# Later attention units: k and q transposed in place, their low parts subtracted by GpSimd

## The chip, the core and the metric

The kernel runs on one core of one Trainium2 chip. The metric is device microseconds of one execution. Three runs of the kernel before took 695.42, 696.80 and 697.27 us: a median of 696.8 us.

## What is computed

Inputs are q, k and v of 4 batches x 8 heads x 768 positions x 64, and two weight matrices, 512 x 2048 and 2048 x 512, stored as 64-bit floats. First comes a linear attention with a decay for each head, then a two-layer network with softplus:

```python
for t in range(S):
    state = gamma[None, :, None, None] * state + np.einsum('bhd,bhe->bhde', k[:, :, t], v[:, :, t])
    y[:, :, t] = scale * np.einsum('bhd,bhde->bhe', q[:, :, t], state)
x = np.ascontiguousarray(y.transpose(0, 2, 1, 3)).reshape(B * S, H * D)
h = x @ w_in
g = np.maximum(h, 0.0) + np.log1p(np.exp(-np.abs(h)))
out = (g @ w_out).astype(np.float32)
```

## The kernel before

**Attention by units.** A unit is 128 positions (a chunk) of four of the eight heads: 4 batches x 6 chunks x 2 halves = 48 units. The recurrence is done chunk by chunk: scores of the chunk (`sc`), masked to the lower triangle (`ah`, `al`), times v, plus q times the state that the chunks before left (`st`); the sum is `yp`, and the state grows by k times v (`stp`). The decays are multiplied into q and v beforehand by GpSimd (L166 or L162, and L167). The first chunk of a batch has no state to read.

**Hi and lo parts.** TensorE multiplies most things as fp32r, a shortened fp32. A value is split into a rounded high part (a cast on ACT) and a low part (value minus high part), and a product is three products: high-high, high-low, low-high. The first 12 units do without this in attention (their k and q are transposed by TensorE, L176). The 36 later units, those that the change touches, load k and q a second time as blocks of 32 x 32 (`kb`, `qb`: 16 DMAs of 16 KB for a unit, L136), so that DVE's 32 x 32 transpose puts each block in its place.

**A later unit, before.** DVE transposes `kb` and `qb` into one PSUM tile `tp` (L184). ACT casts high parts of k and q into `kq` (L187, L188), which has two buffers, `kq0` and `kq1`, for even and odd units; DVE subtracts to get the low parts (L190, L191). `kq` index 0 holds k (high part on a head's own 64 partitions, low part on the other 64), index 1 q's high part on both, index 2 q's low part. TensorE makes the scores in two steps of two heads (L212); ACT and DVE split them (L214 to L216); GpSimd masks `ah`, then `al` (L218); TensorE makes `yp` (L284 to L288); ACT and DVE split it into the ring `xh`, `xl` (L290, L292), from which the first layer reads.

**PSUM.** `tp`, the two `sc` tiles and `yp` of a unit all come from one pool with two buffers of one bank each, taken in turn in the order in which the program asks: `sc`, `sc`, `tp` of the next unit, `yp`.

**The two layers.** Rows are processed in nine blocks (2 x 256, 6 x 384, 256). A step makes 512 columns' worth of the hidden layer: 12 products `hp` for a 384 block (L320 to L322), a softplus chain DVE, ACT, DVE (L327, L328, L332), the split (ACT `gh` L334, GpSimd `gl` L336), and two steps later nine products `acc` of the second layer (L351 to L353). `hp` has two buffers. A block's first two steps can do half of their `hp` products before the last unit of the block has its `yp`, and the other half after.

**The order.** The program emits the parts of a unit at ticks between the steps, and Tile's scheduler, which runs its own timeline, sets the order of each engine's queue. Each engine then works through its queue in that order, and an instruction that waits holds what stands behind it. All the large loads are issued by SP's queue (SyncE), in one order as well. A block tile has two buffers, so the blocks of a unit can be loaded when those of the unit two earlier are free.

Of the kernel before, what the change touches and what calls it, by code (L numbers as in the profile page):

```python
# [10 lines left out]
F32 = mybir.dt.float32  # L11
# [4 lines left out]
ALU = mybir.AluOpType  # L16

P = 128
C = 128
# [14 lines left out]
def decay_attention_then_softplus_ffn(ctx: ExitStack, tc: tile.TileContext, q, k, v, w_in, w_out, qtab, vtab, gtab, out):  # L34
    nc = tc.nc
# [9 lines left out]
    NJ = HH // 2  # L45
# [6 lines left out]
    ps_a = ctx.enter_context(tc.tile_pool(name="ps_a", bufs=2, space=bass.MemoryType.PSUM))  # L52
# [116 lines left out]
    def operands(n):  # L169
        b, c, hf = units[n]  # L170
        kn, *rest, vn = loads.pop(n)
        tp = ps_a.tile([P, 2, NJ, C], F32, name="tp", tag="a")
        if n < WHOLE:
            for t, x in enumerate((kn, *rest)):
                for j in range(NJ):
                    nc.tensor.transpose(tp[:, t, j, :], x[:, 2 * j:2 * j + 2, :], ident)  # L176
            qt = qs[:, n % 2]
            nc.scalar.copy(kz[lo, 0], tp[lo, 0])
            nc.vector.tensor_copy(kz[up, 1], tp[up, 0])
            nc.scalar.copy(qt, tp[:, 1])  # L180
            live[n] = [qt, kn, vn]
            return
        for t, x in enumerate(rest):
            nc.vector.transpose(tp[:, t].rearrange("p j c -> p (j c)"), x.rearrange("p m i d -> p (m i d)"))  # L184
        kq = kqs[n % 2]
        for par, own, oth in sides:
            nc.scalar.copy(kq[own, :2, par], tp[own])  # L187
            nc.scalar.copy(kq[oth, 1, par], tp[own, 1])  # L188
        for par, own, oth in sides:
            nc.vector.tensor_tensor(kq[oth, 0, par], tp[own, 0], kq[own, 0, par].bitcast(F32), op=ALU.subtract)  # L190
            nc.vector.tensor_tensor(kq[own, 2, par], tp[own, 1], kq[own, 1, par].bitcast(F32), op=ALU.subtract)  # L191

        vhl = attn.tile([P, HH, 2, D], F32R, name="vhl", tag="vhl", bufs=2)
        nc.scalar.copy(vhl[:, :, 0, :], vn)
        nc.vector.tensor_tensor(vhl[:, :, 1, :], vn, vhl[:, :, 0, :].bitcast(F32), op=ALU.subtract)
        live[n] = [kq, vhl, kn, vn]
# [100 lines left out]


    PARTS = {-6: load_unit, -2: decay, 0: operands, 2: scores, 3: new_state, 5: stack_and_outputs}
    FIRST_TICK = min(PARTS)  # L300
    PERIOD = 4
# [72 lines left out]
    for i, a, b in turns:  # L374
        m = WIDE // BLOCKS[i]
# [64 lines left out]
    for a, b in zip(starts, starts[1:]):  # L440
        i = steps[b][0]
        if i == 2:
            a = b - SPREAD
        have = ticks_for(i - 1)
        for s in range(a, b):

            t, n = (s - a + 1, b - a) if i == 2 else (min(s - a, b - a - 2), b - a - 2)
# [59 lines left out]
```

## Time and profile before

| | before |
|---|---|
| median of 3 runs | 696.8 us (695.42 to 697.27) |
| profiled execution | 699.58 us, span 697.8 us |
| TensorE busy | 663.9 us, 95% of the span |
| VectorE (DVE) busy | 419.7 us, 60% |
| ScalarE (ACT) busy | 343.4 us, 49% |
| GpSimd (POOL) busy | 283.1 us, 41% |
| DMA | 47.53 MB, mean 68 GB/s |

The profile names engines PE (TensorE products), PEld (its weight loads), DVE, ACT, POOL and SP. A row of a group gives the line of the kernel, the engine and operation, output <- inputs, shapes and count, then busy us and mean ns of one, then how long the engine stood idle just before and what ended that. A row of the timeline gives start, duration, and in brackets the idle time before and its releaser. TensorE's products overlap: the distance between two starts, not the duration, is what one costs in a dense stretch. The first 100 us load and convert the weights; the later units run from about 110 us to 610 us; then only the two layers are left.

### The profile page before, as it was taken

The page shows a single profiled execution, that of the slowest core. Times are in us where ns is not written, and L with a number is a line of the kernel's source. Part 1 is how long each engine was busy: PE and PEld are TensorE (multiplying, and loading weights), DVE is VectorE, ACT ScalarE, POOL GpSimd, SP SyncE. Part 2 cuts the span into 40 slices and gives each one's busy share as a digit, 9 for nine tenths or more (in the row PEclk, how much of TensorE's full clock was granted, in tenths as well). Part 3 has the DMA queues.
Part 4 walks back from the last instruction along what each step waited for, and adds up shares of the span by engine and source line. Part 5 has one row for each costly group of instructions (what it writes and reads, how often), then busy time and mean ns, then how long its engine had stood idle before and what let it go on. Part 6 is the DMA issues. An engine that isn't in the chain of part 4 may idle for free.

```text
span 697.8 us, 12577 instructions
## 1 busy us (share of the span) xinstructions
PE 663.9 (95%) x4136; PEld 602.5 (86%) x4136; DVE 419.7 (60%) x915; ACT 343.4 (49%) x772; POOL 283.1 (41%) x354
## 2 busy tenths in 40 slices
PE   5798899999999999998999979999899998999997
PEld 4787899998999889997999879998799988999996
DVE  5675777567556676666666666664865666543321
ACT  4866766455445455454444455443644536432221
POOL 5766677333333244333333424343243324222221
PEclk9998999999999999999999999999999999999999
DMA  8788750232112331122212232122221231000100
GB/s 245 210 217 230 213 167 23 41 85 64 35 33 40 75 80 36 25 44 72 38 33 43 37 95 56 22 45 40 74 37 33 41 73 41 1 1 1 46 0 31
DMA packets 156993, 47.53 MB, mean 68 GB/s; under 512 B 143616, under 2 KB 151808, under 8 KB 156928
## 3 DMA queue, kind: packets, MB, share of 16 engines
q1 hardware_dynamic: 156480, 46.72, 28.0%
q8 instruction: 33, 0.54, 0.3%
q14 instruction: 32, 0.26, 0.1%
q10 hardware_dynamic: 448, 0.01, 0.0%
HBM read 40.39 MB, written 6.29 MB: 67 GB/s over the span
## 4 chain that ended last, share of the span: by engine, by line
PE 82%; DMA 7%; DVE 3%; ACT 3%; SPq 2%; POOL 1%; issue 1%; DVEq 0%; POOLq 0%; ACTq 0%
PE hp L320 12%; PE hp L322 12%; PE hp L321 12%; PE acc L352 12%; PE acc L351 12%; PE acc L353 11%; PE sc L212 2%; PE stp L235 2%; DMA win<-in_moe_w_in_dram 2%; DMA wout<-in_moe_w_out_dram 2%; PE yp L287 1%; DMA vn<-in_v_dram 1%; SPq L136 1%; PE yp L288 1%; PE yp L286 1%
## 5 line engine op out<-in xcount | busy, mean ns | idle before, releaser
L336 POOL TENSOR_TENSOR gl<-sp,gh 128x384 fp32r<-128x384 f32 (+1 forms) x120 | 128.7, 1074 | 174.4 <-ACT gh L334 157.7
L320 PE MATMUL hp<-xh,winhl 128*128 128x384 f32 (+1 forms) x576 | 187.8, 328 | 2.9 <-DMA out_dram<-o 2.4
L322 PE MATMUL hp<-xh,winhl 128*128 128x384 f32 (+1 forms) x576 | 185.9, 323 | 0.3 <-POOL winhl L99 0.3
L321 PE MATMUL hp<-xl,winhl 128*128 128x384 f32 (+1 forms) x576 | 185.3, 322 | 0.0
L351 PE MATMUL acc<-wouthl,gh 128*128 128x512 f32 x384 | 151.3, 395 | 0.0
L352 PE MATMUL acc<-wouthl,gh 128*128 128x512 f32 x384 | 151.3, 394 | 0.0
L353 PE MATMUL acc<-wouthl,gl 128*128 128x512 f32 x384 | 147.9, 395 | 0.1
L327 DVE TENSOR_SCALAR sp<-hp 128x384 uint32<-128x384 uint32 (+1 forms) x120 | 69.2, 578 | 95.6 <-PE hp L322 90.0
L328 ACT ACTIVATE sp<-sp 128x384 f32<-128x384 f32 (+1 forms) x120 | 65.4, 546 | 120.7 <-DVE sp L327 120.5
L320 PEld LDWEIGHTS hp<-xh,winhl 128*128 128x128 f32 x576 | 109.7, 191 | 7.7 <-ACT xh L290 3.5
L321 PEld LDWEIGHTS hp<-xl,winhl 128*128 128x128 f32 x576 | 110.2, 191 | 3.5
L334 ACT CAST gh<-sp 128x384 fp32r<-128x384 f32 (+1 forms) x120 | 63.9, 534 | 97.9 <-DVE sp L332 69.8
L322 PEld LDWEIGHTS hp<-xh,winhl 128*128 128x128 f32 x576 | 110.0, 191 | 0.6 <-POOL winhl L99 0.5
L332 DVE SCALAR_TENSOR_TENSOR sp<-hp,sp 128x384 f32<-128x384 f32 (+1 forms) x120 | 69.2, 579 | 29.5 <-ACT sp L328 28.9
L353 PEld LDWEIGHTS acc<-wouthl,gl 128*128 128x128 f32 x384 | 71.3, 188 | 14.3 <-POOL gl L336 0.5
L351 PEld LDWEIGHTS acc<-wouthl,gh 128*128 128x128 f32 x384 | 72.2, 188 | 11.3
L352 PEld LDWEIGHTS acc<-wouthl,gh 128*128 128x128 f32 x384 | 72.2, 188 | 11.1
L218 POOL TENSOR_SCALAR_AFFINE_SELECT ah<-ah 128x512 fp32r<-128x512 f32 (+1 forms) x48 | 30.6, 637 | 125.3 <-DVE al L215 119.9
L187 ACT CAST kq<-tp 64x512 fp32r<-64x512 f32 x72 | 41.8, 580 | 26.9 <-DVE tp L184 26.2
L190 DVE TENSOR_TENSOR kq<-tp,kq 64x256 fp32r<-64x256 f32 x72 | 30.4, 422 | 33.6 <-ACT kq L188 32.8
L166 POOL TENSOR_TENSOR qb<-qb,qblocks 128x256 f32<-128x256 f32 x36 | 22.3, 621 | 58.2 <-DMA qb<-in_q_dram 52.1
L292 DVE TENSOR_TENSOR xl<-yp,xh 64x256 fp32r<-64x256 f32 x72 | 30.0, 416 | 21.7 <-ACT xh L290 20.7
(79 smaller groups left out, 974.8 us busy)
## 6 DMA issues: line engine op xcount, KB each, us to landing
win<-in_moe_w_in_dram SPq DMA_DIRECT2D x16, 512.0 KB, 4.7
wout<-in_moe_w_out_dram SPq DMA_DIRECT2D x16, 512.0 KB, 4.3
kn<-in_k_dram SPq DMA_DIRECT2D x48, 128.0 KB, 2.3
vn<-in_v_dram SPq DMA_DIRECT2D x48, 128.0 KB, 2.3
out_dram<-o SPq DMA_DIRECT2D x24, 256.0 KB, 2.1
kb<-in_k_dram SPq DMA_DIRECT2D x288, 16.0 KB, 1.7
qb<-in_q_dram SPq DMA_DIRECT2D x288, 16.0 KB, 1.7
qn<-in_q_dram SPq DMA_DIRECT2D x12, 128.0 KB, 4.0
```

The source lines that it names most:

```text
L187: nc.scalar.copy(kq[own, :2, par], tp[own])
L320: nc.tensor.matmul(hp[:, k], lhsT=wt[:, 0, d, :], rhs=xh[:, d, :], start=d == 0, stop=False)
L321: nc.tensor.matmul(hp[:, k], lhsT=wt[:, 0, d, :], rhs=xl[:, d, :], start=False, stop=False)
L322: nc.tensor.matmul(hp[:, k], lhsT=wt[:, 1, d, :], rhs=xh[:, d, :], start=False, stop=d == ND - 1)
L327: nc.vector.tensor_scalar(sp.bitcast(U32), hps[s].bitcast(U32), 0x80000000, None, op0=ALU.bitwise_or)
L328: nc.scalar.activation(sp, sp, AF.Softplus)
L332: nc.vector.scalar_tensor_tensor(g, hps.pop(s), 0.0, g, op0=ALU.max, op1=ALU.add)
L334: nc.scalar.copy(gh, g)
L336: nc.gpsimd.tensor_tensor(gl, sps.pop(s), gh.bitcast(F32), op=ALU.subtract)
L351: nc.tensor.matmul(acc[i][t], lhsT=gh[:, k, ts], rhs=wt[:, 0], start=begins and k == 0, stop=False)
L352: nc.tensor.matmul(acc[i][t], lhsT=gh[:, k, ts], rhs=wt[:, 1], start=False, stop=False)
L353: nc.tensor.matmul(acc[i][t], lhsT=gl[:, k, ts], rhs=wt[:, 0], start=False, stop=ends and f == fs[-1])
```

## The change

For the 36 later units, `kb` and `qb` are transposed in place in SBUF, and `tp` is not asked for. ACT casts from the transposed blocks, one 64 x 256 piece at a time, k first, then q: six casts for a unit instead of four. GpSimd makes all four low parts of a unit, from the transposed block and the high part, both in SBUF. Since k and q have instructions of their own now, k's part can stand at another place in the queues than q's. A block's buffer is free once its subtractions are done, where before it was free after the transpose. Nothing else in the source differs.

```diff
     def operands(n):
         b, c, hf = units[n]
         kn, *rest, vn = loads.pop(n)
-        tp = ps_a.tile([P, 2, NJ, C], F32, name="tp", tag="a")
         if n < WHOLE:
+            tp = ps_a.tile([P, 2, NJ, C], F32, name="tp", tag="a")
...
-        for t, x in enumerate(rest):
-            nc.vector.transpose(tp[:, t].rearrange("p j c -> p (j c)"), x.rearrange("p m i d -> p (m i d)"))
+        for x in rest:
+            blocks = x.rearrange("p m i d -> p (m i d)")
+            nc.vector.transpose(blocks, blocks)
+        kt, qt = (x.rearrange("p m i d -> p m (i d)") for x in rest)
         kq = kqs[n % 2]
         for par, own, oth in sides:
-            nc.scalar.copy(kq[own, :2, par], tp[own])
-            nc.scalar.copy(kq[oth, 1, par], tp[own, 1])
+            nc.scalar.copy(kq[own, 0, par], kt[own])
+            nc.gpsimd.tensor_tensor(kq[oth, 0, par], kt[own], kq[own, 0, par].bitcast(F32), op=ALU.subtract)
         for par, own, oth in sides:
-            nc.vector.tensor_tensor(kq[oth, 0, par], tp[own, 0], kq[own, 0, par].bitcast(F32), op=ALU.subtract)
-            nc.vector.tensor_tensor(kq[own, 2, par], tp[own, 1], kq[own, 1, par].bitcast(F32), op=ALU.subtract)
+            nc.scalar.copy(kq[own, 1, par], qt[own])
+            nc.scalar.copy(kq[oth, 1, par], qt[own])
+            nc.gpsimd.tensor_tensor(kq[own, 2, par], qt[own], kq[own, 1, par].bitcast(F32), op=ALU.subtract)
```

Lines behind this move by three: L212 becomes L215, L218 becomes L221, L284 to L288 become L287 to L291, L290 becomes L293, L320 to L322 become L323 to L325, L336 becomes L339. The scheduler orders the queues anew. In the rows below the number behind a name is that of the buffer or tile, which tells two tiles of one name apart.

TensorE where the first layer of block 4 begins (blocks count from 0; the turn near 325 us in the trace before), from the last products of that block's last attention unit, `yp_3741` before:

```order
L287 MATMUL yp_3741<-al_3671,vhl_3571 64x128
L288 MATMUL yp_3741<-ah_3670,vhl_3571 64x128
L353 MATMUL acc0_3026<-wouthl_1340,gl_3853 128x512
L353 MATMUL acc1_3027<-wouthl_1340,gl_3853 128x512
L352 MATMUL acc2_3028<-wouthl_1340,gh_3851 128x512
L353 MATMUL acc2_3028<-wouthl_1340,gl_3853 128x512
L320 MATMUL hp_3864<-xh_82,winhl_245 128x384
L320 MATMUL hp_3894<-xh_82,winhl_303 128x384
L212 MATMUL sc_3815<-kq0_84 128x256 x2
```

The same place after (there the last unit's output is `yp_3756`):

```order
L290 MATMUL yp_3756<-al_3685,vhl_3585 64x128
L291 MATMUL yp_3756<-ah_3684,vhl_3585 64x128
L323 MATMUL hp_3879<-xh_82,winhl_245 128x384
L323 MATMUL hp_3909<-xh_82,winhl_303 128x384
L215 MATMUL sc_3830<-kq0_84 128x256 x2
L324 MATMUL hp_3879<-xl_83,winhl_245 128x384
```

Four products of the second layer no longer stand between the unit's `yp` and the first product that reads its `xh`; they stand earlier. Block 6 begins in the same way, both before and after.

GpSimd at the same turn, before: the masks of the block's last unit (`ah_3670`, `al_3671`) and of the unit after it (`ah_3807`, `al_3808`):

```order
L336 TENSOR_TENSOR gl_3782<-sp_3776,gh_3780 128x384
L218 AFFINE_SELECT ah_3670<-ah_3670 128x512
L218 AFFINE_SELECT al_3671<-al_3671 128x512
L336 TENSOR_TENSOR gl_3853<-sp_3847,gh_3851 128x384
L166 TENSOR_TENSOR qb_3795<-qb_3795,qblocks_80 128x256
L167 TENSOR_TENSOR vn2_92<-vn2_92,vtabs_79 128x4x64
L218 AFFINE_SELECT ah_3807<-ah_3807 128x512
L218 AFFINE_SELECT al_3808<-al_3808 128x512
```

And after, where the same two units have `ah_3684` and `ah_3822`:

```order
L166 TENSOR_TENSOR qb_3810<-qb_3810,qblocks_80 128x256
L190 TENSOR_TENSOR kq1_85<-kb_3663,kq1_85 64x256
L194 TENSOR_TENSOR kq1_85<-qb_3672,kq1_85 64x256
L167 TENSOR_TENSOR vn2_92<-vn2_92,vtabs_79 128x4x64
L190 TENSOR_TENSOR kq1_85<-kb_3663,kq1_85 64x256
L221 AFFINE_SELECT ah_3684<-ah_3684 128x512
L194 TENSOR_TENSOR kq1_85<-qb_3672,kq1_85 64x256
L221 AFFINE_SELECT al_3685<-al_3685 128x512
L190 TENSOR_TENSOR kq0_84<-kb_3801,kq0_84 64x256 x2
L221 AFFINE_SELECT ah_3822<-ah_3822 128x512
L221 AFFINE_SELECT al_3823<-al_3823 128x512
```

Subtractions for later units now stand in front of, and between, the masks that `yp` waits for. `kq1` holds the operands of the unit whose mask is `ah_3684` and of the unit two later, so the first of these rows can run only once `sc` of the former is made.

ACT where block 3 begins (near 244 us before), from the `st` casts to the split of the last unit's `yp`. Before, it reads:

```order
L334 CAST gh_2879<-sp_2875 128x384
L255 CAST st1_2786<-stp_93 64x128 x2
L290 CAST xh_82<-yp_2761 64x2x128 x2
L214 CAST ah_2835<-sc_2837 128x256
L194 CAST vhl_2954<-vn0_90 128x4x64
```

And after:

```order
L368 COPY o_2979<-acc1_2029 128x512
L192 CAST kq1_85<-qb_2686 64x256
L193 CAST kq1_85<-qb_2686 64x256
L192 CAST kq1_85<-qb_2686 64x256
L258 CAST st1_2795<-stp_93 64x128 x2
L193 CAST kq1_85<-qb_2686 64x256
L293 CAST xh_82<-yp_2770 64x2x128 x2
L217 CAST ah_2844<-sc_2846 128x256
```

Four casts of a later unit's q, which wait until `yp_2770` no longer reads `kq1`, now stand ahead of the two that copy `yp_2770` out.

In SP's queue the `kb` transfers of units 14 and 15 (16 DMAs) move forward, in between the loads of the weights; before, they stood behind the last of these.

## The prediction

> **What bounds the kernel now.** I read the page's head first, then the chain of waits, then busy time by stage, then TensorE's own waits, and at last the instructions around one of those waits. The page, and two of my three stages (us, then busy us and instructions of each engine, TensorE's granted clock, DMA share and GB/s):
>
> ```profile
> span 697.8 us, 12577 instructions
> PE 663.9 (95%) x4136; PEld 602.5 (86%) x4136; DVE 419.7 (60%) x915; ACT 343.4 (49%) x772; POOL 283.1 (41%) x354
> PE 82%; DMA 7%; DVE 3%; ACT 3%; SPq 2%; POOL 1%; issue 1%; DVEq 0%; POOLq 0%; ACTq 0%
> 0.00:110.00 110.00, 92.29 (x626) 83.95 (x627) 75.42 (x141) 74.26 (x150) 74.10 (x97) 0.97 0.74 205
> 110.00:620.00 510.00, 497.45 (x3065) 451.77 (x3064) 321.92 (x737) 249.63 (x588) 191.43 (x242) 0.99 0.22 46
> ```
>
> TensorE is the bound: 95% of the span, and 82% of the chain that ended last. Between 110 and 620 us, where the changed units run, it idles 510.00 - 497.45 = 12.6 us. Its number of products does not change, so a gain there can be at most these 12.6 us; a loss has no such ceiling. Who holds it up (us in total, times, longest):
>
> ```profile
> PE yp L284 <- DVE al L216: 5.0, 5, 1.1
> PE yp L287 <- POOL al L218: 3.7, 6, 1.4
> PE hp L320 <- DMA out_dram<-o: 2.4, 2, 1.2
> PE sc L212 <- DVE xl L292: 1.2, 3, 0.5
> PE sc L212 <- DVE al L216: 0.3, 1, 0.3
> ```
>
> These add up to 12.6 us, and only code of later units waits here, so this is all of that stage's idle time. Asked by stretches, the waits fall at six places only, the turns from one block of rows into the next (blocks 2 to 7, near 162, 244, 325, 410, 486 and 570 us): 0.5, 1.5, 1.8, 3.5, 1.8 and 3.3 us. At a turn the first layer of the new block needs the attention of its last unit, and the matrix work that could fill the time has run out. The turn near 325 us, and the one wait near 405 us that has nothing to fill it (start, duration, then idle time and releaser in brackets):
>
> ```profile
> 320.59 0.75 ACT L290 CAST xh<-yp 64x256 fp32r<-64x256 f32 x2 [4.54 <-PE yp L288]
> 321.48 0.84 DVE L292 TENSOR_TENSOR xl<-yp,xh 64x256 fp32r<-64x256 f32 x2
> 322.46 0.47 PE L212 MATMUL sc<-kq 128*128 128x256 f32 x2 [0.45 <-DVE xl L292]
> 323.94 0.64 POOL L218 TENSOR_SCALAR_AFFINE_SELECT ah<-ah 128x512 fp32r<-128x512 f32 x1 [2.79 <-DVE al L215]
> 325.74 0.64 POOL L218 TENSOR_SCALAR_AFFINE_SELECT al<-al 128x512 fp32r<-128x512 f32 x1 [1.16 <-DVE al L216]
> 325.75 0.24 PE L284 MATMUL yp<-kq,st 128*64 128x128 f32 x1 [1.07 <-DVE al L216]
> 326.43 0.27 PE L287 MATMUL yp<-al,vhl 128*64 128x128 f32 x1 [0.31 <-POOL al L218]
> 405.12 0.62 PE L320 MATMUL hp<-xh,winhl 128*128 128x384 f32 x2 [1.21 <-DMA out_dram<-o]
> ```
>
> The chain of a turn: `yp` is copied out (ACT, then DVE), only then has the second `sc` a bank, its scores go through ACT and DVE, GpSimd masks both halves, and the next `yp` may go on. GpSimd is already the last link (L287). The releaser named at 405 us is long done; by the code L320 waits there for `xh`.
>
> **The change, part by part.** Durations, from the groups by shape, and three ACT rows in order of time:
>
> ```profile
> L187 ACT CAST kq<-tp 64x512 fp32r<-64x512 f32 x72 | 41.8, 580 | 26.9 <-DVE tp L184 26.2
> L188 ACT CAST kq<-tp 64x256 fp32r<-64x256 f32 x72 | 26.5, 367 | 1.1
> L194 ACT CAST vhl<-vn 128x256 fp32r<-128x256 f32 x36 | 14.7, 408 | 0.3
> L190 DVE TENSOR_TENSOR kq<-tp,kq 64x256 fp32r<-64x256 f32 x72 | 30.4, 422 | 33.6 <-ACT kq L188 32.8
> L191 DVE TENSOR_TENSOR kq<-tp,kq 64x256 fp32r<-64x256 f32 x72 | 30.4, 422 | 1.0
> L184 DVE STREAM_TRANSPOSE tp<-kb 128x256 f32<-128x256 f32 x36 | 16.4, 457 | 1.2 <-DVE al L215 0.2 <-DVE sp L332 0.2
> L167 POOL TENSOR_TENSOR vn<-vn,vtabs 128x256 f32<-128x256 f32 x48 | 29.5, 616 | 18.4 <-DMA vn<-in_v_dram 16.5 <-ACT gh L334 1.3 <-PE acc L353 0.4
> L336 POOL TENSOR_TENSOR gl<-sp,gh 128x384 fp32r<-128x384 f32 x96 | 97.6, 1018 | 126.8 <-ACT gh L334 111.4 <-DMA qb<-in_q_dram 4.3 <-issue 4.2
> L410 POOL MEMSET kq<- 64x256 f32 x4 | 1.2, 306 | 0.1
> 328.78 0.54 ACT L255 CAST st<-stp 64x128 fp32r<-64x128 f32 x2
> 330.11 0.41 ACT L194 CAST vhl<-vn 128x256 fp32r<-128x256 f32 x1
> 330.42 0.51 ACT L334 CAST gh<-sp 128x384 fp32r<-128x384 f32 x1
> ```
>
> *Engine time.* DVE loses 144 subtractions: 60.8 us. GpSimd gains 144. No GpSimd subtraction of 64x256 is in the trace; below, it cannot be cheaper than the 0.31 us fill of that shape, above, not dearer than the 1.02 us of `gl` at 128x384 (group L336), which is larger; I take 0.62 us, the two-input product with the same 256 elements per partition. That is 89 us, 12% of the span more on a queue busy 41%. The Trainium skill ("GPSIMD Engine Reference", 4.1 Engine selection) puts a two-input elementwise operation at about twice VectorE's time, which speaks against the move; the rows here give 616 / 422 = 1.46, and at twice, 0.84 us, the sum below would grow by about 2 us. ACT goes from 2 x (0.580 + 0.367) to 6 x 0.41 us per unit, 20 us in all. The transpose keeps its 0.46 us whether it writes PSUM or SBUF (bounds 0.42, the DVE's rows of that size, to 0.69, its 512-wide rows). None of these engines is full; all this is hidden under TensorE (497 of 510 us) unless it lands on the chain of a turn, where it costs its full time.
>
> *Reload of the blocks.* `qb` is now free only after GpSimd's last subtraction instead of after the transpose, and the next decay L166 waits for its reload in GpSimd's own queue.
>
> ```profile
> 314.43 3.69 SPq L136 DMA_DIRECT2D qb<-in_q_dram  x8
> 319.41 0.62 POOL L166 TENSOR_TENSOR qb<-qb,qblocks 128x256 f32<-128x256 f32 x1 [1.95 <-DMA qb<-in_q_dram]
> 309.15 0.60 PE L235 MATMUL stp<-vn,kn 128*128 128x128 f32 x4
> 309.51 0.42 PE L320 MATMUL hp<-xh,winhl 128*128 128x384 f32 x1
> 311.94 0.39 PE L351 MATMUL acc<-wouthl,gh 128*128 128x512 f32 x1
> 314.02 0.33 PE L320 MATMUL hp<-xh,winhl 128*128 128x384 f32 x1
> 315.09 0.39 PE L351 MATMUL acc<-wouthl,gh 128*128 128x512 f32 x1
> ```
>
> From first issue to decay: 319.41 - 314.43 = 5.0 us. The order after puts subtraction, one `gl` (1.0), decay: so GpSimd stands about 4 us per unit, with the next unit's k subtractions and the masks behind it. TensorE's pitch: nine `acc` 2.08 us, six `hp` 1.07, four `stp` 0.36. Inside a block the order has about 12.7 us of products between one `yp`'s end and the first of the next that needs `ah`; GpSimd's sequence after that end (q copies and subtractions 1.6, reload 5.0, decay 0.6, k subtractions 1.2, mask 0.6) is ready at 9.0. Margin 3.7 us: hidden. If that cover were gone, each of some 24 such units would pay the difference.
>
> *The turns*, where nothing covers. With state (into 3, 5, 7) ACT runs four q copies and the two `st` casts ahead of `xh`: 4 x 0.31 (330.11 to 330.42, the pitch above) + 0.54 (L255) + 0.75 (L290), less 0.3 already running under the last products: `xh` is whole 2.2 us after `yp`. Into 3 only `stp` (0.36) fills: 1.85 idle, 0.2 more for `sc`'s bank, and the old wait of the next `yp`, 1.3: 3.3 against 1.5. Into 5 and 7, six `acc` (1.39) and `stp` fill, which the order before did not have there: 0.45 + 0.2 + 1.3 = 1.95 against 3.5 and 3.3. First chunk of a batch (into 4 and 6; 2 too): no state is read, but GpSimd gets two k and one q subtraction and `vn` ahead of `ah`, one more ahead of `al`. Into 4, from `sc`'s end: copies 0.4, then 4 x 0.62, mask 0.64, 0.62, 0.64: `al` at 4.75; the ten `hp` products last 1.8 and the other `sc` 0.24, so 2.7 idle. Then `yp` is followed at once by L320: 1.2 (the 405 us row), 0.6 for the bank, and 1.3 as before: 5.8 against 1.8. Into 6, 4.25 us of `acc` and `hp` stand in between: 0.3 + 1.2 + 0.6 + 1.3 = 3.4 against 1.8. Into 2: 0.5 as now.
>
> *The head.* Sixteen `kb` transfers of units 14 and 15 move from about 119 us into the weight loads (55 to 75 us), in a queue that took 5.5 us for eight of them there:
>
> ```profile
> 83.26 5.52 SPq L136 DMA_DIRECT2D qb<-in_q_dram  x8
> 119.26 4.38 SPq L136 DMA_DIRECT2D kb<-in_k_dram  x8
> ```
>
> That is 11 us of issue in a queue with 2 to 4 us gaps between weight loads. Bounds 0 and 5; I take 1.0.
>
> *Sum.* Turns: 0.5 + 3.3 + 5.8 + 1.95 + 3.4 + 1.95 = 16.9 against 12.4: +4.5. Head +1.0. Inside blocks 0. The profiled execution took 699.58 us (span 697.8 and 1.8 around it); with +5.5 it would take 705.1. It lies 2.8 us above the median of the runs shown, 696.8, so for a median I say **702.3 us**.
>
> **Rivals.**
> *The bank pays.* Without `tp`, `yp` takes the bank of the first `sc`, not of the second. The L284 wait (5.0 us) goes, and DVE, 61 us lighter, serves `sp` and `al` sooner. For: GpSimd's select at 325.74 started 0.15 us after DVE's end. Against: L287 then waits for that same select. At best L284, L212 and part of L287 go, 5.0 + 1.5 + 1.5 = 8: about 691 to 694.
> *Nothing shows.* The two waits trade and the head does not move: 696 to 698. For: all engines but TensorE are under 62%.
> *GpSimd's queue becomes the bound (slower).* If a subtraction takes 1.0 us instead of 0.62 and the reload 7 us, the margin of 3.7 falls to 3.7 - 2.0 - 0.8 = 0.9; late `gl` and head-of-line waits eat that, from where some 24 units lose 0.5 to 1 us each: 12 to 24 more, 714 to 726. Against: 41% + 12% busy.
> *DVE held by GpSimd.* The `vhl` subtraction has two SBUF inputs and stands between the `al` steps:
>
> ```profile
> L195 DVE TENSOR_TENSOR vhl<-vn,vhl x36: 414/425/1272, 124.1 to 604.1; 128x256 fp32r<-128x256 f32 x36
> ```
>
> Usually 0.42 us, 1.27 at worst, and the long ones began as a GpSimd `gl` ran. With more GpSimd work it may be held at each of five turns: 5 x 0.85 = 4.2, that is 706.5. The Trainium skill ("SBUF — State Buffer", Who interferes with whom) states it as a lock: such an instruction and a GpSimd one that reads SBUF exclude each other. By that rule, the trace agrees.
>
> **How the numbers follow.** Forecast 0.40, DVE held on top 0.08, queue bound 0.10, nothing shows 0.20, bank pays 0.22. Differences under 0.3% (2.1 us: 694.7 to 698.9) cannot be told from none here. Slower: most of forecast (0.35), 0.08, 0.10, little of the third: 0.54. Same: 0.05 + 0.17: 0.22. Faster: the rest, 0.24. The forecast alone spans 698 to 707 (subtraction 0.31 to 1.02 us moves the turns by -2 to +3, head 0 to 5); 8 in 10 needs the bank's end and the lower part of the queue's: 692 to 714.
>
> **What would show it.** Right: TensorE's idle between 110 and 620 us near 17 us, with L215 or L323 waiting for `xl`/`xh` at the turns into 3, 4 and 6, and L289/L290 for GpSimd's masks; shorter waits into 5 and 7; POOL L166 idle for `qb` near 4 us a unit; subtractions at 0.62 us; DVE about 61 us less busy. Wrong: idle under 12 us (the bank pays), or waits inside blocks (queue bound), or the loss before 110 us (head).

## The result, and the profile after

The changed kernel takes **702.67 us** (median of 5 runs, 701.53 to 704.13), where the kernel before took 697.27 (5 runs beside it on the same chip). The ratio is 1.008, with a 95% interval of 1.0058 to 1.0102: slower by 5.4 us. The forecast was 702.3, within 692 to 714. Of the experiments below, one of the five executions of "VectorE subtracts" took 753.95 us, with the clock granted at 0.838; the ratio in the table leaves it out, the median does not.

The page after: span, and busy time of each engine.

```profile
span 701.3 us, 13055 instructions
PE 666.4 (95%) x4136; PEld 604.0 (86%) x4136; DVE 357.5 (51%) x771; ACT 362.5 (52%) x844; POOL 387.6 (55%) x498
```

VectorE's busy time fell by 62 us, ScalarE's grew by 19 and GpSimd's by 104. The same two stages as shown of before (us, then busy us and instructions of PE, PEld, DVE, ACT and POOL, then TensorE's granted clock, DMA share and GB/s):

```profile
0.00:110.00 110.00, 93.84 (x637) 85.52 (x638) 77.94 (x147) 79.50 (x162) 79.71 (x105) 0.97 0.76 206
110.00:620.00 510.00, 494.92 (x3025) 448.27 (x3024) 256.31 (x585) 262.87 (x646) 289.26 (x377) 0.99 0.22 46
```

TensorE idles 15.1 us in the later units (12.6 before) and 16.2 in the head (17.7 before). Its busy time grew by 2.5 us with the same 4136 products. The span grew by 3.5 us (701.3 against 697.8): 2.5 of idle time in the later units, 2.5 of busy time, and 1.5 less in the head. The profiled execution took 702.99 us against 699.58. TensorE's waits between 110 and 620 us (total, times, longest):

```profile
PE yp L289 <- POOL ah L221: 4.4, 3, 3.0
PE stp L238 <- DVE st L260: 3.7, 3, 2.6
PE yp L290 <- POOL al L221: 2.5, 4, 0.9
PE hp L323 <- ACT xh L293: 1.7, 2, 0.8
PE sc L215 <- DVE xl L295: 1.1, 3, 0.4
PE sc L215 <- DVE al L219: 1.0, 2, 0.5
PE hp L323 <- DVE sp L335: 0.5, 1, 0.5
```

Before, `yp` waited first for VectorE's `al` (5.0 us); that wait is gone, and GpSimd's masks and the state's copies stand in its place. The worst turn is that into block 4; GpSimd's queue there, and the two waits of TensorE for it (start, duration, idle time and releaser in brackets):

```profile
320.51 0.62 POOL L166 TENSOR_TENSOR qb<-qb,qblocks 128x256 f32<-128x256 f32 x1 [4.12 <-DMA qb<-in_q_dram]
321.20 0.73 POOL L190 TENSOR_TENSOR kq<-kb,kq 64x256 fp32r<-64x256 f32 x1
322.00 0.71 POOL L194 TENSOR_TENSOR kq<-qb,kq 64x256 fp32r<-64x256 f32 x1
322.69 0.60 POOL L167 TENSOR_TENSOR vn<-vn,vtabs 128x256 f32<-128x256 f32 x1
323.37 0.72 POOL L190 TENSOR_TENSOR kq<-kb,kq 64x256 fp32r<-64x256 f32 x1
324.16 0.63 POOL L221 TENSOR_SCALAR_AFFINE_SELECT ah<-ah 128x512 fp32r<-128x512 f32 x1
324.88 0.73 POOL L194 TENSOR_TENSOR kq<-qb,kq 64x256 fp32r<-64x256 f32 x1
325.68 0.63 POOL L221 TENSOR_SCALAR_AFFINE_SELECT al<-al 128x512 fp32r<-128x512 f32 x1
324.85 0.28 PE L289 MATMUL yp<-ah,vhl 128*64 128x128 f32 x1 [3.00 <-POOL ah L221]
326.37 0.37 PE L290 MATMUL yp<-al,vhl 128*64 128x128 f32 x1 [0.95 <-POOL al L221]
```

The scores of `ah` were split by 321.9 (VectorE's first `al` step of that half ran from 321.53 to 321.92), but the mask starts at 324.16, behind three subtractions and a decay of later units, and the mask of `al` is behind one more. The queue was late already: the decay in the first row had waited 4.12 us for its reload and ended at 321.13, while ScalarE's first cast of the new k (L189) had ended at 320.39, so the first subtraction could have begun some 0.7 us sooner.

The granted clock explains part of the busy time that grew. The same turn, in three stretches:

```profile
322.00:326.00 4.00, 0.57 (x3) 0.37 (x3) 0.97 (x2) 0.65 (x2) 3.69 (x6) 1.00 0.29 96
326.00:333.00 7.00, 5.80 (x24) 5.17 (x25) 3.65 (x9) 2.98 (x8) 2.42 (x5) 0.52 0.21 33
333.00:337.00 4.00, 4.00 (x37) 3.96 (x37) 2.05 (x5) 2.91 (x9) 2.90 (x4) 0.98 0.20 33
```

After the stall TensorE is granted 0.52 of its clock for 7 us; 5.8 us of products there cost about 2.8 us more than at full clock (5.80 x 0.48). The kernel before has stretches of this kind too, behind its longest stalls, into blocks 5 and 7:

```profile
412.00:416.00 4.00, 4.00 (x19) 4.00 (x17) 2.26 (x6) 2.52 (x8) 1.97 (x2) 0.57 0.20 31
579.00:583.00 4.00, 4.00 (x19) 4.00 (x18) 2.26 (x6) 2.81 (x8) 1.97 (x2) 0.57 0.18 29
```

As an estimate, busy time times the missing share of the clock, added up over windows of 1 us, is 6.0 us before and 7.5 after. That is 1.5 of the 2.5 us; the other 1.0 is not explained.

### The profile page after: what moved, and what is told of

The parts are those of the page before. It is cut to its first block, busy times and chain, and to the rows that moved or that the text cites. A ratio compares the mean times of both kernels' runs of the same rounds, so it can differ in the third digit from the quotient of the medians.

```text
span 701.3 us, 13055 instructions
## 1 busy us (share of the span) xinstructions
PE 666.4 (95%) x4136; PEld 604.0 (86%) x4136; DVE 357.5 (51%) x771; ACT 362.5 (52%) x844; POOL 387.6 (55%) x498
## 4 chain that ended last, share of the span: by engine, by line
PE 77%; DMA 5%; POOL 4%; ACT 3%; issue 3%; SPq 3%; DVE 2%; POOLq 0%; ACTq 0%; DVEq 0%
PE hp L323 11%; PE hp L324 11%; PE hp L325 11%; PE acc L355 11%; PE acc L354 11%; PE acc L356 11%; SPq L136 2%; PE sc L215 2%; PE stp L238 2%; DMA win<-in_moe_w_in_dram 1%; POOL kq L190 1%; PE yp L290 1%; PE yp L291 1%; PE yp L289 1%; POOL kq L194 1%
## 5 line engine op out<-in xcount | busy, mean ns | idle before, releaser
L339 POOL TENSOR_TENSOR gl<-sp,gh 128x384 fp32r<-128x384 f32 (+1 forms) x120 | 129.4, 1080 | 180.8 <-ACT gh L337 156.6
L323 PE MATMUL hp<-xh,winhl 128*128 128x384 f32 (+1 forms) x576 | 186.8, 327 | 3.4 <-ACT xh L293 1.7
L325 PE MATMUL hp<-xh,winhl 128*128 128x384 f32 (+1 forms) x576 | 185.5, 322 | 0.0
L323 PEld LDWEIGHTS hp<-xh,winhl 128*128 128x128 f32 x576 | 109.4, 191 | 8.6 <-ACT xh L293 2.0
L325 PEld LDWEIGHTS hp<-xh,winhl 128*128 128x128 f32 x576 | 109.7, 190 | 0.4
L356 PEld LDWEIGHTS acc<-wouthl,gl 128*128 128x128 f32 x384 | 71.7, 188 | 14.8 <-POOL gl L339 0.5
L194 POOL TENSOR_TENSOR kq<-qb,kq 64x256 fp32r<-64x256 f32 x72 | 52.8, 733 | 31.9 <-ACT kq L192 24.6
L190 POOL TENSOR_TENSOR kq<-kb,kq 64x256 fp32r<-64x256 f32 x72 | 53.0, 736 | 25.4 <-ACT kq L189 20.6
L185 DVE STREAM_TRANSPOSE kb<-kb 128x256 f32<-128x256 f32 x36 | 16.0, 444 | 66.9 <-DMA kb<-in_k_dram 40.0
L192 ACT CAST kq<-qb 64x256 fp32r<-64x256 f32 x72 | 29.0, 403 | 33.2 <-PE yp L287 26.7
L295 DVE TENSOR_TENSOR xl<-yp,xh 64x256 fp32r<-64x256 f32 x72 | 30.0, 417 | 22.7 <-ACT xh L293 21.8
```

The costliest lines, as they stand in the source:

```text
L190: nc.gpsimd.tensor_tensor(kq[oth, 0, par], kt[own], kq[own, 0, par].bitcast(F32), op=ALU.subtract)
L323: nc.tensor.matmul(hp[:, k], lhsT=wt[:, 0, d, :], rhs=xh[:, d, :], start=d == 0, stop=False)
L325: nc.tensor.matmul(hp[:, k], lhsT=wt[:, 1, d, :], rhs=xh[:, d, :], start=False, stop=d == ND - 1)
L339: nc.gpsimd.tensor_tensor(gl, sps.pop(s), gh.bitcast(F32), op=ALU.subtract)
L356: nc.tensor.matmul(acc[i][t], lhsT=gl[:, k, ts], rhs=wt[:, 0], start=False, stop=ends and f == fs[-1])
```

## Experiments

Three questions: do the queue positions at the turns make the loss, as predicted; what is the freed bank worth; what is it worth that GpSimd, not VectorE, subtracts? Each run is compared with runs of the kernel before on its own chip; that kernel's medians lay between 696.6 and 697.8. The summary, with TensorE's idle time between 110 and 620 us, its busy time and mean granted clock in the profiled execution:

| kernel | median us | ratio to before, 95% | idle | busy | clock |
|---|---|---|---|---|---|
| before | 697.3 | 1 | 12.6 | 663.9 | 0.990 |
| the change | 702.7 | 1.008 [1.0058, 1.0102] | 15.1 | 666.4 | 0.988 |
| masks first | 694.4 | 0.9959 [0.994, 0.9978] | 10.2 | 664.2 | 0.988 |
| xh first | 691.5 | 0.9908 [0.9886, 0.993] | 6.8 | 663.4 | 0.990 |
| both first | 680.5 | 0.9755 [0.9731, 0.9778] | 0.9 | 657.7 | 0.995 |
| bank held | 704.2 | 1.0094 [1.0069, 1.0119] | 15.6 | 667.4 | 0.988 |
| xh first, bank held | 692.7 | 0.994 [0.9916, 0.9964] | 8.2 | 661.6 | 0.993 |
| both first, bank held | 679.5 | 0.9756 [0.9722, 0.979] | 2.3 | 659.7 | 0.991 |
| VectorE subtracts | 722.9 | 1.0358 [1.0333, 1.0382] | 23.3 | 674.3 | 0.979 |
| VectorE subtracts, xh first | 705.9 | 1.0117 [1.0086, 1.0148] | 13.4 | 668.5 | 0.983 |
| VectorE subtracts, both first | 705.4 | 1.0115 [1.0084, 1.0147] | 15.5 | 669.6 | 0.987 |
| xh first, subtracted twice | 716.9 | 1.0282 [1.025, 1.0313] | 19.8 | 672.0 | 0.986 |
| both first, subtracted twice | 685.0 | 0.9832 [0.9796, 0.9869] | 3.6 | 659.4 | 0.997 |

### The order at the turns

A rule on the order is a dependency that orders two instructions of one engine and adds no wait:

```python
def hold(late, early, why):
    tc.add_manual_dep(late.ins, early.name, mybir.DependencyInfo(mybir.DependencyClass.NoSync, mybir.DependencyReason.DATA), reason=why)
```

**Masks first.**

```diff
-            nc.gpsimd.tensor_tensor(kq[oth, 0, par], kt[own], ...)
+            low = nc.gpsimd.tensor_tensor(kq[oth, 0, par], kt[own], ...)
+            hold(low, masked[n - 2], "masks first")
```

and the same for q's low part; `masked[n]` is the last mask of unit n.

> The change with one rule on the order more: GpSimd's subtractions of a unit come after the masks of the unit two before it. Nothing else is asked for. My theory: the waits of yp for GpSimd's masks into blocks 4 and 6 (3.0 + 0.95 and 0.94 + 1.07 us) fall to what the kernel before has there, about 1 us each; the waits for st and xh into 3, 5 and 7 stay; idle in the middle 15.1 to about 12, time 699 to 700.5. Rival, re-ordered products: no smaller idle, 701 to 704. Rival, GpSimd's queue is short of time: subtractions that come later make the next unit's scores late, sc waits for kq, 704 to 708.

**xh first.**

```diff
-            nc.scalar.copy(kq[own, 1, par], qt[own])
-            nc.scalar.copy(kq[oth, 1, par], qt[own])
+            for half in (own, oth):
+                hold(nc.scalar.copy(kq[half, 1, par], qt[own]), split[n - 2], "xh first")
```

`split[n]` is the last cast of unit n to `xh`.

> The change with one rule on the order more: ScalarE's q casts of a unit come after the casts to xh of the unit two before it. My theory: the wait of stp for st into block 3 (2.55 us in the changed kernel, with q casts ahead of st) and its smaller kind into 5 and 7 (0.6 each) go, the waits for the masks into 4 and 6 stay or grow by under 1 us as the q subtractions come later; idle in the middle 15.1 to 11.5 to 12.5, time 699 to 700.5. Rival, the order is bounded elsewhere (the state's copies are late by themselves): idle unchanged, 702 to 703. Rival, later q casts make q's low part and so the next scores late: 704 to 708.

**Both.**

> The change with both rules: GpSimd's subtractions of a unit after the masks of the unit two before, and ScalarE's q casts after the casts to xh of that unit. With the xh rule alone the changed kernel took 691.5 us and waited 2.6 us for ah from GpSimd and 4.0 us for scores' banks in the middle; with the masks rule alone 694.4. Theory (two separate causes at separate turns): the masks' wait of 2.6 us goes as well, time 689 to 691. Rival (the two rules cure the same thing, a late order of the whole turn): no better than the xh rule alone, 691 to 693. Rival (subtractions held back come too late for the next scores): 693 to 697.

Measured: 694.4, 691.5 and 680.5 us. All three fell further than the theory said: the first two were put at 699 to 700.5, the third at 689 to 691. The theory counted idle time alone; from "xh first" to both, TensorE's idle time fell by 5.9 us and its busy time by 5.7. What is left of TensorE's waits tells the two causes apart. With masks first (lines move by eight):

```profile
PE sc L223 <- DVE xl L303: 7.3, 3, 2.9
PE yp L297 <- POOL ah L229: 2.2, 2, 1.4
PE yp L298 <- POOL al L229: 0.3, 1, 0.3
```

The three long waits are the turns into 3, 5 and 7 (239.82, 405.03 and 571.99 us, at 2.01, 2.87 and 2.46). ScalarE's rows ahead of the first show the cause, four q casts and `st` ahead of `xh`:

```profile
233.30 0.41 ACT L199 CAST kq<-qb 64x256 fp32r<-64x256 f32 x1 [0.86 <-PE yp L295]
233.73 0.41 ACT L200 CAST kq<-qb 64x256 fp32r<-64x256 f32 x1
234.16 0.40 ACT L199 CAST kq<-qb 64x256 fp32r<-64x256 f32 x1
234.59 0.53 ACT L266 CAST st<-stp 64x128 fp32r<-64x128 f32 x2
235.15 0.40 ACT L200 CAST kq<-qb 64x256 fp32r<-64x256 f32 x1
235.57 0.74 ACT L301 CAST xh<-yp 64x256 fp32r<-64x256 f32 x2
```

With xh first, no wait for `st` or `xh` is left (lines move by six):

```profile
PE sc L221 <- DVE al L225: 3.8, 4, 1.7
PE yp L295 <- POOL ah L227: 2.6, 2, 1.3
PE sc L221 <- DVE xl L301: 0.2, 1, 0.2
PE yp L296 <- POOL al L227: 0.2, 1, 0.2
```

With both, one wait is left in 510 us:

```profile
PE sc L223 <- DVE al L227: 0.6, 1, 0.6
```

ScalarE at the turn into 3 and GpSimd at the turn into 4 now stand as the rules ask, `xh` ahead of the q casts and the masks ahead of the subtractions:

```profile
232.13 0.74 ACT L301 CAST xh<-yp 64x256 fp32r<-64x256 f32 x2
232.90 0.37 ACT L225 CAST ah<-sc 128x256 fp32r<-128x256 f32 x1
233.16 1.69 ACT L200 CAST kq<-qb 64x256 fp32r<-64x256 f32 x4
...
319.67 0.64 POOL L229 TENSOR_SCALAR_AFFINE_SELECT ah<-ah 128x512 fp32r<-128x512 f32 x1 [3.60 <-DVE al L226]
320.40 0.64 POOL L229 TENSOR_SCALAR_AFFINE_SELECT al<-al 128x512 fp32r<-128x512 f32 x1
321.12 1.55 POOL L196 TENSOR_TENSOR kq<-kb,kq 64x256 fp32r<-64x256 f32 x2
```

By ratio the rules are worth 1.2% and 1.7% alone and 3.25% together: 8.4, 12.0 and 22.7 us. They cure separate waits, so the rival that they cure one thing falls. The kernel before has ScalarE's casts behind `xh` already, and VectorE's subtractions behind the additions to `al`: the corresponding rules, put on it, leave the order of every engine as it is. So the change, with these two kinds of instruction in the order that the old kernel had anyway, is 17 us faster than before; without the rules it was slower, with the new instructions placed ahead of the turn's chain.

One thing is not separated. Under each rule the scheduler also re-laid TensorE's products (about half of its positions differ, or more), so how much comes from the freed queue and how much from products that now fill the turn is open.

### The freed bank

```diff
+        tp = ps_a.tile([P, 2, NJ, C], F32, name="tp", tag="a")
+        nc.vector.memset(tp[:1, 0, 0, :1], 0.0)
         for x in rest:
             blocks = x.rearrange("p m i d -> p (m i d)")
```

The bank is taken in its turn again, for one element of 59 ns. TensorE's order changes in few places, so this is the cleanest of the comparisons. It tells what the turn in the ring is worth; before, `tp` also kept its bank through transposes, casts and subtractions, and what that longer hold cost is not measured. It was done on the change, with xh first, and with both rules.

> The change with the PSUM bank taken again: each later unit takes a tile of the score ring, and VectorE writes one element of it before the transposes; all else is as in the change (transposes in SBUF, GpSimd's subtractions). It tells what the freed bank is worth. My theory (freed bank pays back about 0.9 us at each of the four turns into 3, 4, 5, 6 by ending the old wait for the masks): idle in the middle up by 2 to 4 us, time 704.5 to 707. Rival, the bank is worth nothing: 702 to 703.5. Rival, the freed bank made it worse, since yp and the scores now meet in other banks: 698 to 701.

> The change with the xh rule (691.5 us), and the bank of the score ring taken again as in e6_bank_held. The kernel before has ScalarE's casts in the order of this rule already, so this tells how much of the 5.9 us that the change gains under this order is the bank's. Theory (the bank pays about 1.5 us, as it did without the rule): 692 to 694. Rival (the bank is the gain, hidden by the order without the rule): 695 to 698. Rival (worth nothing, all of it is VectorE's lighter queue): 690.5 to 692.

> The change with both rules (680.5 us), and the bank of the score ring taken again for each later unit. Theory (the bank pays 1.3 to 1.5 us, as in the two pairs measured so far): 681 to 683. Rival (with the order mended the bank is what lets the second scores run early, and pays most of the 17 us): 688 to 696.

Differences of ratio: +0.0014, +0.0032 and +0.0001, or 1.0, 2.2 and 0.1 us, and each pair's intervals overlap. The medians, 704.2, 692.7 and 679.5, lie just under the theory of the first (704.5 to 707; its idle time rose by 0.5 us, not 2 to 4), within that of the second, and below all that was said of the third. In the first pair `yp` waits for the bank itself, which the change does not show:

```profile
PE yp L289 <- DVE tp L184: 1.1, 3, 0.6
```

So the bank's turn is worth a microsecond or two at most by these differences, and no pair tells it from nothing. It is not what gains 17 us.

### VectorE subtracts

```diff
-            nc.gpsimd.tensor_tensor(kq[oth, 0, par], kt[own], ..., op=ALU.subtract)
+            nc.vector.tensor_tensor(kq[oth, 0, par], kt[own], ..., op=ALU.subtract)
```

and the same for q. Done on the change, with xh first, and with both rules (in the last, each subtraction after the last addition to `al` of the unit two before).

> The change with the low parts of k and q subtracted by VectorE again (144 instructions, both inputs in SBUF); the bank stays free and ScalarE still makes six casts per unit. My theory (the loss sits at the turns: GpSimd's subtractions ahead of the masks into blocks 4 and 6, ScalarE's q casts ahead of st and xh into 3, 5 and 7): the waits of yp for ah and al from GpSimd, 7 us in the changed kernel, fall to 2 to 3 us, the waits for st and xh stay; idle between 110 and 620 us falls from 15.1 to about 11, time 698 to 700. Rival, the freed bank is a gain that the GpSimd part hides: idle falls to 7 to 9 and the time below 696. Rival, the loss comes from the re-ordered products of TensorE whatever the engines do: idle 14 to 16, time 701 to 704. VectorE: subtractions 0.42 us each, so it is busy about 418 us again; if two SBUF inputs made it wait for GpSimd, some of them take over 1 us and the mean goes over 0.5.

> The low parts subtracted by VectorE from SBUF as in e1_dve_sub (722.9 us), with the rule that ScalarE's q casts come after the casts to xh. It tells whether that kernel was slow by its order at the turns or by VectorE's subtractions of two SBUF operands, which took 0.52 to 0.58 us on average there and up to 1.4 instead of 0.42 from PSUM. Theory (order): 5 us of its waits for xh and 3 for st go, and with GpSimd as light as before it comes to 694 to 702. Rival (VectorE held by GpSimd): subtractions stay at 0.5 to 0.6 us and the waits for al and xl behind them (8.5 us there) stay, time 705 to 715.

> The change with both rules (680.5 us), but the low parts subtracted by VectorE from SBUF, each after the last addition to al of the unit two before. The kernel before (697.5 us) has all its instructions in the order that these rules ask for, so this tells which part of the 17 us that the change gains under that order comes from GpSimd taking the subtractions. Theory (they are the gain: VectorE's queue at a turn is shorter, and its subtractions of two SBUF operands took 0.46 to 0.57 us where GpSimd was busy): 693 to 702, with VectorE's subtractions at 0.45 us or more. Rival (the freed bank and the transposes in place are the gain): 680 to 686.

Expected of the first was 698 to 700; it took 722.9, by far the largest miss of the study. Undoing this half does not lead back: VectorE's subtractions read PSUM before, and read two SBUF operands now. Minimum, median and maximum ns of one; first two rows of the kernel before, then the first of these three runs:

```profile
L190 DVE TENSOR_TENSOR kq<-tp,kq x72: 417/422/428, 121.7 to 612.3; 64x256 fp32r<-64x256 f32 x72
L191 DVE TENSOR_TENSOR kq<-tp,kq x72: 415/422/428, 122.2 to 612.8; 64x256 fp32r<-64x256 f32 x72
```

```profile
L190 DVE TENSOR_TENSOR kq<-kb,kq x72: 418/421/1387, 46.7 to 614.0; 64x256 fp32r<-64x256 f32 x72
```

And with both rules, where the mean grew most (busy us, mean ns):

```profile
L196 DVE TENSOR_TENSOR kq<-kb,kq 64x256 fp32r<-64x256 f32 x72 | 48.7, 676 | 2.2
L201 DVE TENSOR_TENSOR kq<-qb,kq 64x256 fp32r<-64x256 f32 x72 | 34.9, 485 | 1.5
```

None of 144 took over 0.43 us from PSUM; from SBUF some take up to 1.4. The order is not the whole reason: xh first brings this kernel from 722.9 to 705.9, and the second rule no further (705.4). The 705.9 lies where the rival of a held VectorE put it (705 to 715), not the theory of the order (694 to 702); the 705.4 lies above both the theory (693 to 702) and the rival (680 to 686). Under both rules, GpSimd instead of VectorE is worth 705.4 - 680.5 = 25 us. How much of that is the held subtractions (about 23 us of VectorE's time by the two means above) and how much is VectorE's queue standing for block reloads in front of `o` and `st` copies (66.0 us of VectorE's waits there are for `kb`, against 25.5 where GpSimd subtracts) was not told apart.

### GpSimd's subtractions, done twice

Each subtraction is issued a second time over the same output; the result is unchanged.

> The change with the xh rule (691.5 us), and each of GpSimd's 144 subtractions done twice, the second time over the same output: 106 us more on GpSimd, 2 x 0.73 us more ahead of k's and of q's part of each unit. It tells what the subtractions' time is worth once the order is mended. Theory (they are hidden inside the blocks by some 3 us of margin and cost their time only at the turns, where one or two of them stand on the chain): 693 to 697. Rival (GpSimd's queue sets the pace): each of 36 units 0.5 us later or more, over 705. Rival (wholly hidden): 690.5 to 692.5.

> The change with both rules (680.5 us), and each of GpSimd's subtractions done twice, as in e8_sub_twice, which had the xh rule alone and lost 25 us by it. It tells whether that loss was GpSimd's time as such or the masks queued behind the subtractions. Theory (the masks' place): with the masks first the second subtractions are hidden inside the blocks, 681 to 687. Rival (GpSimd's time as such): over 695, with waits of sc for kq.

Twice the subtractions add 109 us to GpSimd in both. With xh first alone the kernel went from 691.5 to 716.9 us; with the masks first too, from 680.5 to 685.0. The first number misses the theory (693 to 697) and fits the rival (over 705), but the rival's mechanism does not fit: nearly all of the waits are at the turns, the largest being

```profile
PE yp L298 <- POOL al L229: 5.6, 5, 1.2
PE hp L331 <- ACT xh L301: 5.1, 5, 1.2
```

With the masks first, GpSimd is busy 73% of the span and TensorE still loses only 3.6 us of 510, with no wait of the scores for `kq`. That is the theory of the second run (681 to 687). So it is mostly where the subtractions stand in the queue that decides whether their time costs anything.

## Why the prediction was right, and where it was not

**Direction and time: right, the last digits by luck.** 702.3 was said, 702.67 measured. The sum for the profiled execution was less good, 705.1 against 702.99: the profiled execution before lay 2.3 us above its median, that after 0.3, and this covered the difference. Three terms were off and made up for one another in part: +4.5 was said for the turns and +2.4 came, +1.0 for the head and -1.5 came, and nothing for TensorE's busy time, where +2.5 came. What was right is the direction and where the turns lose and gain.

**The turns: the mechanism was right, the sizes partly.** TensorE's idle time by turn:

| into block | 2 | 3 | 4 | 5 | 6 | 7 | sum |
|---|---|---|---|---|---|---|---|
| before | 0.5 | 1.5 | 1.8 | 3.5 | 1.8 | 3.3 | 12.4 |
| forecast | 0.5 | 3.3 | 5.8 | 1.95 | 3.4 | 1.95 | 16.9 |
| after | 0.3 | 3.0 | 4.8 | 1.7 | 3.2 | 1.8 | 14.8 |

The five turns for which a move was forecast moved that way (into 2 none was, and 0.2 us went), and the two rules on the order confirm both causes. Inside three of them the terms differ most.

- Into 3, the wait came for `st` (2.55 us at L238), where 1.85 was put on `xh`: the same q casts stand ahead of both, and TensorE reaches `stp` first. They stood 0.43 us apart (238.16, 238.59 and 239.01), not 0.31. About 0.6 of the 2.55 is VectorE's: ScalarE's casts to `st` had ended at 239.97, but an `o` copy that had waited 3.15 us for its buffer stood ahead of VectorE's step (rows below). The bank (0.2) and the old wait for the masks (1.3) did not come; 0.49 for `sp` did.
- Into 4, GpSimd cost 3.00 + 0.95 where 2.7 was said: `al` was masked 6.2 us after the scores' end, not 4.75. Half of the difference is the late decay shown above (the first subtraction began 1.13 us after the scores, not 0.4), the other half the dearer subtractions and the gaps between the instructions. The wait for `xh` was 0.83, not 1.2. The bank (0.6) and the old wait (1.3) did not come.
- Into 6, 0.94, 0.83, 0.35 and 1.07 came for 0.3, 1.2, 0.6 and 1.3.

VectorE at the turn into 3, after:

```profile
239.85 0.69 DVE L368 COPY o<-acc 128x512 f32<-128x512 f32 x1 [3.15 <-DMA out_dram<-o]
240.57 0.59 DVE L260 TENSOR_TENSOR st<-stp,st 64x128 fp32r<-64x128 f32 x2
```

The over-large term is thus "1.3 as before", kept at five turns: the forecast let the rival of the freed bank count for nothing there, and part of that old wait did go. How much of it is the bank's is open; the three pairs differ by 0.1 to 2.2 us, none of them clear of nothing.

**The subtraction: mis-sized.** 0.62 us was taken, the decay's time at the same 256 elements; it measures 0.736.

```profile
L190 POOL TENSOR_TENSOR kq<-kb,kq 64x256 fp32r<-64x256 f32 x72 | 53.0, 736 | 25.4 <-ACT kq L189 20.6
L166 POOL TENSOR_TENSOR qb<-qb,qblocks 128x256 f32<-128x256 f32 x36 | 22.2, 617 | 29.0 <-DMA qb<-in_q_dram 22.0 <-ACT ah L217 2.0 <-ACT sp L331 1.5
```

The row to extrapolate from was `gl`, with two full operands, not the decay, whose second operand repeats one number over 32 elements. Two shapes of `gl` after, 1026 ns at 384 elements and 1294 at 512, give 2.1 ns per element, and so about 0.76 us at 256. That is 1.75 times VectorE's 0.42, between the 1.46 that was read from the decay and the 2 of the Trainium skill ("GPSIMD Engine Reference", 4.1 Engine selection).

**The reload: smaller on the whole, but not harmless at the turns.** "Near 4 us per unit" was said for L166's wait for `qb`; the row above has 22.0 us in 36, against 52.1 before. Nothing inside the blocks came to wait, as said, and with the subtractions doubled (3.0 us more a unit) and the masks first next to nothing did either, so a margin of about that size was there. The turns into 4 and 6 are another matter: there the decay waited 4.12 and 5.08 us, and the subtractions and masks stood behind it, which the sum of the turns left out.

**The head: wrong in sign.** +1.0 was said, -1.5 came. The moved transfers cost nothing visible.

**What the sum left out.** TensorE's busy time was held constant. It grew by 2.5 us, some 1.5 of them, by the estimate above, through the granted clock. Since busy time moves too, the statement that a gain "can be at most these 12.6 us" failed: with both rules 11.7 us of idle time went in the later units, TensorE's busy time fell by 6.2 us more, and the head gave 0.6. These make the whole 18.5 us of the two spans.

**The rivals.** *Nothing shows* fell: the interval of the ratio begins at 1.0058. *The bank pays* had the right gain in mind for the wrong reason: a faster kernel was there, but held back by the order, not given by the bank. *GpSimd's queue becomes the bound* did not occur, even at 73% busy. *DVE held by GpSimd* did not show for `vhl`, whose mean fell from 572 to 459 ns; it did show where VectorE had to subtract from SBUF. Here the Trainium skill ("SBUF — State Buffer", Who interferes with whom) says that an instruction of VectorE with two SBUF inputs and a GpSimd one that reads SBUF shut each other out, and one with a PSUM input does not: maxima of 1387 and 428 ns for the same subtraction agree.

**What the prediction could not see.** It took the order of the changed program as part of the change, and priced that. That was right for the time asked, but the cause lies one level up: with both rules the change is worth -17 us, and the placement without them, with the products that the scheduler re-laid along with it, costs about 23 (1.008 against 0.9755).

## What to carry to other kernels

When work moves to another engine under a scheduler, look first at what the new instructions stand in front of at the places where the bounding engine has nothing else to do; two order-only dependencies turned a loss of 0.8% into a gain of 2.45% without touching the work. Price a stall of the bounding engine by more than its length, since the clock behind it counts too. Undoing one half of a change is no way back if the other half has changed where its operands live.

## What the hardware showed beyond expectation

**Stalls cost the clock, though not one for one.** After the 3.00 and 0.95 us waits into block 4, TensorE's clock was granted at 0.52 over 7 us, then 0.98 (rows above). Over the thirteen kernels of the table TensorE's busy time goes from 657.7 us (0.9 us idle) to 674.3 (23.3 us idle), about 0.7 us of busy time per microsecond of idle time, for the same 4136 products. By the estimate used above, the lower clock accounts for 2.8 us in the first and 12.8 in the second, 10 of the 16.6; the rest is open. Only one execution of each kernel was profiled, and executions of the kernel before alone show mean clocks from 0.988 to 0.998. The Trainium skill ("TensorE: Matmul & The Clock Gate", Part 1) describes a gate that passes half of the clock after an idle window of about 3.4 us and all of it after a busy window as long. The half rate agrees. The idle time was shorter here: the trace after shows a stretch at half clock behind a single wait of 2.55 us, into block 3 (row below), and before, the stretch into block 5 came behind waits of 0.95 and 1.36 us. After, the waits of 0.94, 0.83, 0.35 and 1.07 us into block 6 had none behind them, so what decides is not shown.

```profile
241.00:244.00 3.00, 2.78 (x11) 2.79 (x12) 2.41 (x7) 1.61 (x5) 0.19 (x1) 0.50 0.44 128
```

**Two operations of GpSimd at 256 elements a partition differ in price.** The decay, whose second operand repeats one number, takes 617 ns, the subtraction with two full operands 736, though the first runs on 128 partitions and the second on 64. They also differ in operation (multiply, subtract) and output type (f32, fp32r), so it is not shown that the operand makes the difference.

**VectorE's subtraction depends on where its operand lies.** 422 and 421 ns at the median from PSUM and from SBUF, but at most 428 from PSUM and up to 1387 from SBUF beside a busy GpSimd.
